# Layer norm sums by chunks on TensorE, with another order list, in a kernel of interleaved memory-attention and local-attention layers

## The chip, the core and the metric

The kernel runs on one core of one Trainium2 chip. The metric is device time in microseconds (us) from launch to the last result. The time before is the median of three runs. A profile is one execution, recorded instruction by instruction; its span runs from the first to the last instruction.

The core has TensorE (PE in the profile; its weight loads are listed apart as PEld), VectorE (DVE), ScalarE (ACT), GpSimd (POOL) and SyncE (SP), which here issues the loads of weights. Each takes its own instructions in program order and waits on semaphores for the others.

## The reference

Four layers run one after the other over a sequence of 2048 rows of 640: A, B, A, B, each on the layer norm of its input and added to it.

```python
x = x + _A_ref(_layernorm(x), A_mem0, A_Wq, A_Wk, A_Wv, A_Wo, A_seg_len)
x = x + _B_ref(_layernorm(x), B_wqkv, B_wo)
x = x + _A_ref(_layernorm(x), A_mem0, A_Wq, A_Wk, A_Wv, A_Wo, A_seg_len)
x = x + _B_ref(_layernorm(x), B_wqkv, B_wo)

def _layernorm(x, axis=-1, eps=1e-05):
    m = jnp.mean(x, axis=axis, keepdims=True)
    v = jnp.var(x, axis=axis, keepdims=True)
    return (x - m) / jnp.sqrt(v + eps)
```

Layer A walks over 64 segments of 32 rows. To each it puts 8 memory rows in front, projects these 40 rows to q, k and v with 32 heads of 192, does masked attention within the 40 rows, and projects back to 640. The first 8 rows of the result are the memory of the next segment, so the segments are a recurrence. Layer B is local attention, 32 heads of 20, each row looking at 8 rows at a distance of 2, with projections of 640 to 1920 and back.

## The kernel before

**Two lanes and steps.** Activations are kept transposed: features on the 128 partitions, in `NC` = 5 chunks, rows along the free dimension. The first pair of layers works on segment t in lane 0 while the second pair works on segment t - 2 (`LAG`) in lane 1, so one matmul serves both lanes: 80 columns in layer A (2 x 40), 64 in layer B and in a layer norm (2 x 32). `step(t)` does layer A for step t and layer B for step t - 1. There are 66 steps with layer A and a last one with layer B alone. Steps 0, 1, 64 and 65 have one lane only, and so matmuls of 40 columns.

**The list.** What a step issues, and in which order, is written out by hand in `ORDER`; every engine takes its own instructions in this order. In layer A, the heads are done in eight quads i of four heads: `Ki`, `Qi`, `Vi` are projections of 30 matmuls (L303), `KEi`, `QEi`, `VEi` bring them out of PSUM (ACT L329, DVE L335 and L337, ACT L342), `Ti` and `TEi` transpose V (PE L349, DVE L357 and L358), `Si` are the scores (L368), `Ei` the exponential (ACT L374), `EMi` the mask (DVE L380), `POi` probabilities times V (L401), `Ri` the reciprocal of the denominators (ACT L388 and L390), `OT1i` and `OT2i` the normalized output (DVE L408, L413, L414), and `Oai`, `Obi` the two halves of the projection back (15 matmuls each, L420). The last quad's projection is cut into `O7x` (chunks 0 to 2), `O7y` and `O7z` (chunks 3 and 4). Then `MEMa` and `MEMb` copy the new memory rows into `hT` for the next step (DVE L454, one for chunks 0 to 2, one for 3 and 4), and `X1` adds the residual (DVE L510).

Names that begin with a small letter are layer B of the step before: `bsq`, `bst`, `bmv`, `br`, `bap` are its layer norm; `bq`, `bk`, `bv` its projections (25 matmuls of 64 columns each, L523 and L548); `bqE`, `bkE`, `bvE` bring them out; `bs0`, `bs1`, `be0`, `be1`, `eb0`, `eb1` are scores, exponentials and masks; `bt`, `btE` transpose V; `bp`, `on` are the output and its normalization; `bo`, `boE` its transpose (PE L618 to L621, ACT L626); `by` the projection back (L634) and `byE` the residual (DVE L644, L647), which writes lane 1's input of the next step.

**The layer norms.** `LSQ`, `lst`, `LMV`, `LR`, `LAP` make layer A's layer norm for the next step, from `xin`, which `byE` and a copy on GpSimd fill. `LSQ` (`ln_sq`) works on VectorE: it squares the input (L460), sums input and squares over the five chunks in two reductions (L463), and splits the float sums into two bf16 halves, high (L465) and rest (L466). `lst` (`ln_stats`) sums these over the partitions on TensorE by two matmuls with a matrix of ones, each of 128 columns: 64 sums and 64 sums of squares. `LMV` (DVE L480, L482, L483) makes mean and variance, `LR` (ACT L490, L492) the factor, and `LAP` (DVE L500, L502 twice) applies them and writes `hT`. Layer B's `bsq`, `bst`, `bmv`, `br`, `bap` call the same functions on `x1` and write `h2T`. There are 66 of each kind in a run.

At the turn of a step, the first matmuls of `K0` need `LAP` and `MEMa`; its blocks for chunks 3 and 4 need `MEMb`.

**PSUM and weights.** Results of TensorE take four banks in turn (`big`), one pair of banks for `POi`, and two for the accumulators of the projection back. Layer A's weights are 128 pieces of 224 or 256 KB. `resident_pieces` spreads over the list which pieces are loaded anew in every step, from the list and a table of times: 79 (`N_RES`) are kept, 49 go through a ring of eight buffers (`RING`). SP issues each load where the list first uses the piece, as soon as the ring buffer is free. Layer B's weights stay; they are loaded in step 1, in four parts, behind `bst`, `bap`, `bqE` and `bvE`. Input loads and output stores sit on ScalarE's queue behind `QE0`.

```python
PIECE = (8, 7)
...
def big(self, name, shape=(P, 512), dt=F32):
    self.n_big += 1
    return self.ps_one.tile(list(shape), dt, name=name, tag=f"big{self.n_big % 4}")
```

Of the kernel before, what the change touches and what calls it, by code (L numbers as in the profile page):

```python
# [10 lines left out]
BF16 = mybir.dt.bfloat16  # L11
F32 = mybir.dt.float32
ACT = mybir.ActivationFunctionType
ALU = mybir.AluOpType
# [3 lines left out]
P = 128  # L18
D = 640
NC = 5  # L20
# [7 lines left out]
NX = 2 * SEG  # L28
# [16 lines left out]


ORDER = """
K0 Q0 bsq K0y QE0 KE0 V0 bst bmv VE0 Q1 S0 K1 T0 QE1 br bap E0 TE0 KE1 V1 S1 EM0 Q3 PO0 VE1 QE3 E1 bq T1 R0 K2
KE2 bqE TE1 Q2 K3 V2 QE2 OT10 S2 KE3 bk EM1 OT20 S3 PO1 VE2 E2 bkE Q4 T2 EM2 bs1 E3 QE4 V3 R1 K4 TE2 be1 VE3
Q5 OT11 OT21 KE4 PO2 R2 EM3 T3 eb1 bs0 be0 V4 QE5 Oa0 VE4 bv TE3 OT12 OT22 bvE Q6 S4 PO3 eb0 E4 bt R3 QE6 btE  # L50
K5 T4 EM4 K6 KE5 TE4 bp0 V5 OT13 Ob0 OT23 KE6 on0 S5 bp1 VE5 PO4 T5 Oa1 E5 R4 on1 TE5 V6 bo Q7 EM5 OT14 S6 boE
OT24 VE6 Ob1 E6 QE7 PO5 T6 EM6 TE6 by byE R5 K7 KE7 V7 S7 VE7 OT15 E7 OT25 LSQ PO6 EM7 Oa2 R6 T7 Ob2 Oa3 TE7
Ob3 OT16 OT26 Oa5 PO7 Oa6 R7 lst LMV Ob5 Oa4 Ob6 OT17 LR OT27 Ob4 LAP O7x O7y MEMa O7z MEMb X1
""".split()


# [58 lines left out]
class Kernel:  # L115
# [338 lines left out]
            nc.vector.tensor_copy(out=h[:, :, ls, 0:NM], in_=a[:, :, ls, 0:NM])  # L454

    def ln_sq(self, x):

        nc = self.nc
        sq = self.bp.tile([P, NC, NX], BF16, name="sq", tag="sq")
        nc.vector.tensor_tensor(out=sq[:], in0=x[:], in1=x[:], op=ALU.mult)  # L460
        s = self.bp.tile([P, 2, NX], F32, name="ln_s", tag="xc")
        for j, v in enumerate((x, sq)):
            nc.vector.tensor_reduce(out=s[:, j, :], in_=v[:].rearrange("p c n -> p n c"), op=ALU.add, axis=mybir.AxisListType.X)  # L463
        hl = sq[:].rearrange("p c n -> p (c n)")[:, 0:4 * NX].rearrange("p (j a n) -> p j a n", j=2, a=2)
        nc.vector.tensor_copy(out=hl[:, 0], in_=s[:])  # L465
        nc.vector.tensor_tensor(out=hl[:, 1], in0=s[:], in1=hl[:, 0], op=ALU.subtract)  # L466
        return hl

    def ln_stats(self, hl):
        nc = self.nc  # L470
        ps = self.big("ps_st")
        for j in range(2):
            nc.tensor.matmul(ps[:, 0:2 * NX], lhsT=self.ones[:], rhs=hl[:, j].rearrange("p a n -> p (a n)"), start=(j == 0), stop=(j == 1))  # L473
        return ps

    def ln_mv(self, ps):
# [201 lines left out]
    def l_piece(self, n, nt):  # L678
        x = self.xin[nt % 2]
        if n == "LSQ":  # L680
            self.asq = self.ln_sq(x)
        elif n == "lst":
            self.asp = self.ln_stats(self.asq)
        elif n == "LMV":
            self.amv = self.ln_mv(self.asp)
        elif n == "LR":
            self.amr = self.ln_r(self.amv)
        else:
            self.ln1_apply(nt)

    def b_piece(self, n, b):
        k, g = n[:2], n[2:]
        if n == "bsq":
            self.bsq = self.ln_sq(self.x1)
        elif n == "bst":
            self.bsp_ = self.ln_stats(self.bsq)
        elif n == "bmv":
            self.bmv = self.ln_mv(self.bsp_)
        elif n == "br":
            self.bmr = self.ln_r(self.bmv)  # L700
        elif n == "bap":
            self.b_ln_apply(b)
        elif n == "bq":
            self.bqp = self.b_proj(0, "ps_bq")
        elif n == "bqE":
            self.b_qE()
        elif n == "bk":
            self.bkp = self.b_proj(1, "ps_bk")
        elif n == "bkE":
            self.b_kE(b)  # L710
        elif n == "bv":
            self.b_v()
        elif n == "bvE":
            self.b_vE(b)
        elif n == "bt":
            self.b_t()
        elif n == "btE":
            self.b_tE(b)
        elif n == "bo":
            self.b_ot()  # L720
        elif n == "boE":
            self.b_oE()
        elif n == "by":
            self.b_wo()
        elif n == "byE":
            self.b_yE(b)
        elif k == "bs":
            self.b_s(int(g))
        elif k == "be":
            self.b_e(int(g))  # L730
        elif k == "eb":
            self.b_m(b, int(g))
        elif k == "bp":
            self.b_pv(int(g))
        else:
            assert k == "on", n
            self.b_on(int(g))
# [115 lines left out]
```

## Time and profile before

| what | value |
|---|---|
| median of 3 runs | 3143.12 us (3140.52 to 3145.89) |
| the profiled execution | 3140.52 us, span 3138.8 us |
| granted TensorE clock, mean of the span | 0.983 |
| DVE L463, the two reductions of a layer norm | 132 x 701 ns and 132 x some 700 ns |
| DVE L465, L466 | 226 ns and 292 ns, 132 of each |
| PE L473, matmuls with ones | 264, 128 columns each |
| weights loaded through the ring | 3234 loads of 224 or 256 KB, 3.9 to 4.0 us from issue to landing |
| HBM read | 823 MB |

A row of the profile names an engine, a line of the kernel, what is written and read, and the shape. In the timeline, a row is start, length, and the number of instructions merged into it. A matmul's recorded length includes its way through the array, so consecutive matmuls overlap in the record; what one costs in a dense stretch is the distance from start to start.

### The profile page before, as it was taken

How to read it: one execution, taken by the hardware profiler on the slowest of the kernel's cores; microseconds unless marked ns; L12 is line 12 of the kernel's file. 1: busy time of each engine (PE TensorE's matmuls, PEld its weight loads, DVE VectorE, ACT ScalarE, POOL GpSimd, SP SyncE). 2: the span in 40 equal slices, each digit the busy share in tenths (PEclk: the TensorE clock that was granted, in tenths of full speed). 3: DMA queues.
4: the chain of work that ended last, by engine and by line, in shares of the span. 5: the costliest groups of instructions: out<-in, count | busy, mean ns of one | idle time of the engine just before them, and what ended most of it. 6: DMA issues, size and time to landing. Idle time of an engine off the chain costs nothing.

```text
span 3138.8 us, 185804 instructions
## 1 busy us (share of the span) xinstructions
PE 3063.2 (98%) x83160; PEld 3036.4 (97%) x83160; DVE 2358.2 (75%) x6883; ACT 1747.2 (56%) x3829; POOL 48.2 (2%) x162
## 2 busy tenths in 40 slices
PE   6899999999999999999999999999999999999996
PEld 5799999999999999999999999999999999999996
DVE  3577777777777777777777777777777777777775
ACT  2355556555556556556555655555655655655653
POOL 2000000000000000000000000000000000000000
PEclk6899999999999999999999999999999999999998
DMA  9988888888888888888888888888888888888885
GB/s 360 320 263 267 263 262 265 264 264 265 266 268 263 268 266 263 268 266 263 268 266 261 267 263 267 261 265 268 263 267 266 264 267 267 263 269 266 262 274 184
DMA packets 487807, 838.02 MB, mean 267 GB/s; under 512 B 54240, under 2 KB 261984, under 8 KB 487008
## 3 DMA queue, kind: packets, MB, share of 16 engines
q1 hardware_dynamic: 477648, 820.89, 83.2%
q8 instruction: 651, 10.67, 1.4%
q10 hardware_dynamic: 9360, 5.26, 0.6%
q14 instruction: 148, 1.21, 0.1%
HBM read 823.31 MB, written 2.62 MB: 263 GB/s over the span
## 4 chain that ended last, share of the span: by engine, by line
PE 95%; DMA 3%; issue 1%; DVE 1%; ACT 0%; SPq 0%; DVEq 0%; ACTq 0%
PE ps_k L303 18%; PE ps_q L303 18%; PE ps_v L303 18%; PE ps_vt L349 6%; PE ps_o L401 5%; PE ps_s L368 5%; PE ps_by L634 2%; PE ps_bq L523 2%; PE ps_bv L548 2%; PE ps_bk L523 2%; DMA w_ring<-in_wA_dram 1%; PE ps_bs L575 1%; PE ps_bo L598 1%; PE ps_bvt L561 1%; PE ps_st L473 0%
## 5 line engine op out<-in xcount | busy, mean ns | idle before, releaser
L303 PEld LDWEIGHTS <-w_ring 128*128 128x128 bf16 x17754 | 784.4, 100 | 19.4 <-DMA w_ring<-in_wA_dram 10.5
L388 ACT ACTIVATE R<-ps_o 64x320 f32<-64x320 f32 (+1 forms) x1056 | 448.5, 425 | 273.8 <-PE ps_o L401 223.6
L342 ACT CAST VT_140<-ps_v 128x480 bf16<-128x480 f32 (+1 forms) x528 | 288.9, 547 | 230.7 <-PE ps_v L303 227.6
L329 ACT CAST KF_121<-ps_k 128x480 bf16<-128x480 f32 (+1 forms) x264 | 144.1, 546 | 391.2 <-PE ps_k L303 383.3
L374 ACT ACTIVATE Em<-ps_s 80x320 bf16<-80x320 f32 (+1 forms) x528 | 223.3, 423 | 157.2 <-PE ps_s L368 110.7
L420 PEld LDWEIGHTS <-w_ring 128*128 128x128 bf16 x6600 | 291.2, 100 | 3.5 <-DMA w_ring<-in_wA_dram 2.6
L335 DVE CAST QT_127<-ps_q 128x320 bf16<-128x320 f32 (+1 forms) x264 | 127.1, 481 | 203.4 <-PE ps_q L303 203.4
L357 DVE COPY Vt_134<-ps_vt 80x512 bf16<-80x512 bf16 x528 | 219.2, 415 | 71.5 <-PE ps_vt L349 69.3
L349 PE MATMUL ps_vt<-ident,VT_140 128*128 128x128 bf16 x3168 | 267.7, 221 | 0.0
L408 DVE TENSOR_TENSOR OT<-ps_o,R 128x320 bf16<-128x320 f32 (+1 forms) x528 | 249.9, 473 | 22.3 <-ACT R L390 16.6
L329 ACT CAST KF_123<-ps_k 128x480 bf16<-128x480 f32 (+1 forms) x264 | 144.1, 546 | 205.6 <-PE ps_k L303 203.9
L390 ACT ACTIVATE R<-R 128x320 f32<-128x320 f32 (+1 forms) x528 | 244.0, 462 | 16.6
L401 PE MATMUL ps_o<-Em,Vt_134 80*128 80x80 bf16 (+1 forms) x4224 | 238.0, 199 | 1.4 <-issue 1.3
L335 DVE CAST QT_125<-ps_q 128x320 bf16<-128x320 f32 (+1 forms) x264 | 126.5, 479 | 143.1 <-PE ps_q L303 71.9
L349 PEld LDWEIGHTS <-VT_140 128*128 128x128 bf16 x3168 | 191.5, 99 | 0.1
L303 PE MATMUL ps_q<-hT_92,w_ring 128*128 128x80 bf16 (+1 forms) x3234 | 185.8, 201 | 3.7 <-DMA w_ring<-in_wA_dram 2.6
L303 PE MATMUL ps_q<-hT_90,w_ring 128*128 128x80 bf16 (+1 forms) x3234 | 186.3, 201 | 2.2 <-DMA w_ring<-in_wA_dram 1.5
L401 PEld LDWEIGHTS <-Vt_134 80*128 80x128 bf16 x4224 | 181.6, 98 | 1.0 <-issue 0.7
L303 PE MATMUL ps_k<-hT_90,w_ring 128*128 128x80 bf16 (+1 forms) x3003 | 172.7, 201 | 1.4 <-DMA w_ring<-in_wA_dram 0.7
L303 PE MATMUL ps_k<-hT_92,w_ring 128*128 128x80 bf16 (+1 forms) x3003 | 171.8, 201 | 1.4 <-issue 1.4
L380 DVE TENSOR_TENSOR Em<-Em,maskA 80x320 bf16<-80x320 bf16 (+1 forms) x528 | 163.2, 309 | 12.5 <-ACT Em L374 8.4
L414 DVE TENSOR_TENSOR OT<-ps_o,R 64x160 bf16<-64x160 f32 (+1 forms) x528 | 165.1, 313 | 7.3
(3084 smaller groups left out, 8305.2 us busy)
## 6 DMA issues: line engine op xcount, KB each, us to landing
w_ring<-in_wA_dram SPq DMA_DIRECT2D x1716, 256.0 KB, 3.9
w_ring<-in_wA_dram SPq DMA_DIRECT2D x1518, 224.0 KB, 4.0
out_dram<-YT_94 ACTq DMA_DIRECT2D x32, 80.0 KB, 3.7
wqkv_sb<-in_wqkv_dram SPq DMA_DIRECT2D x3, 800.0 KB, 7.7
wo_sb<-in_wo_dram SPq DMA_DIRECT2D x1, 800.0 KB, 7.4
w_k_00_386<-in_wA_dram SPq DMA_DIRECT2D x1, 256.0 KB, 2.8
w_k_10_405<-in_wA_dram SPq DMA_DIRECT2D x1, 256.0 KB, 3.8
w_q_10_438<-in_wA_dram SPq DMA_DIRECT2D x1, 256.0 KB, 4.6
```

Source lines behind the costliest of these rows:

```text
L303: self.nc.tensor.matmul(ps[:, NT * n + c0:NT * n + c1], lhsT=self.block(kind, i, h, k), rhs=hT[:, NT * c + c0:NT * c + c1], start=(h == 0 ...
L329: self.nc.scalar.copy(out=kf[:, :, self.cs], in_=self.kp[i][:, 0:6 * NT].rearrange("p (a n) -> p a n", a=6)[:, :, self.cs])
L335: nc.vector.tensor_copy(out=qt[:, :, 0:4:3, cs], in_=pv[:, :, 0:3:2, cs])
L342: self.nc.scalar.copy(out=vt[:, :, self.cs], in_=self.vp[i][:, 0:6 * NT].rearrange("p (a n) -> p a n", a=6)[:, :, self.cs])
L349: nc.tensor.transpose(out=ps[:, n, :], in_=self.VT[:, NT * n:NT * n + P], identity=self.ident[:])
L357: nc.vector.tensor_copy(out=vt[:, :, 0:4:3, :], in_=src[:, :, 0:3:2, :])
L374: self.nc.scalar.activation(out=e[0:NT, :, cs], in_=self.sv[i][0:NT, :, cs], func=ACT.Exp, scale=float(DH) ** -0.5)
L388: self.nc.scalar.activation(out=r[rows, :, :, self.cs], in_=d, func=ACT.Ln)
L390: self.nc.scalar.activation(out=rf, in_=rf, func=ACT.Exp, scale=-1.0)
L401: nc.tensor.matmul(ov[:, pr, b, self.cs], lhsT=vt[0:NT, 512 * pr + P * b:512 * pr + P * (b + 1)], rhs=em[0:NT, 2 * pr + b // 2, self.cs], ...
L408: self.nc.vector.tensor_tensor(out=ot[:, :, 0:3:2, cs], in0=self.ov[:, :, 0:4:3, cs], in1=self.r[i][:, :, :, cs], op=ALU.mult)
L420: self.nc.tensor.matmul(self.acc[c // 3][:, o:o + self.cs.stop - self.cs.start], lhsT=self.block("o", i, h, k), rhs=ot[:, m, self.cs], sta ...
```

## The change

The change is named so: two DVE copies per quad merged away by a mask on half chunks and wider patterns; 79 resident pieces; list from remeasured DVE times. What differs between the files is this. `ln_sq` only squares. `ln_stats` does the sums over the chunks on TensorE: five matmuls of 64 columns on the input and five on the squares, each with the matrix of ones, added up in PSUM over the chunks. `ORDER` is another list of the same items. `qE`, `tE` and `N_RES` are the same in both files; which 79 pieces stay follows from the list.

```diff
 ORDER = """
-K0 Q0 bsq K0y QE0 KE0 V0 bst bmv VE0 Q1 S0 K1 T0 QE1 br bap E0 TE0 KE1 V1 S1 EM0 Q3 PO0 VE1 QE3 E1 bq T1 R0 K2
-KE2 bqE TE1 Q2 K3 V2 QE2 OT10 S2 KE3 bk EM1 OT20 S3 PO1 VE2 E2 bkE Q4 T2 EM2 bs1 E3 QE4 V3 R1 K4 TE2 be1 VE3
-Q5 OT11 OT21 KE4 PO2 R2 EM3 T3 eb1 bs0 be0 V4 QE5 Oa0 VE4 bv TE3 OT12 OT22 bvE Q6 S4 PO3 eb0 E4 bt R3 QE6 btE
-K5 T4 EM4 K6 KE5 TE4 bp0 V5 OT13 Ob0 OT23 KE6 on0 S5 bp1 VE5 PO4 T5 Oa1 E5 R4 on1 TE5 V6 bo Q7 EM5 OT14 S6 boE
-OT24 VE6 Ob1 E6 QE7 PO5 T6 EM6 TE6 by byE R5 K7 KE7 V7 S7 VE7 OT15 E7 OT25 LSQ PO6 EM7 Oa2 R6 T7 Ob2 Oa3 TE7
-Ob3 OT16 OT26 Oa5 PO7 Oa6 R7 lst LMV Ob5 Oa4 Ob6 OT17 LR OT27 Ob4 LAP O7x O7y MEMa O7z MEMb X1
+K0 bsq Q0 K0y V0 QE0 KE0 bst VE0 Q1 bmv T0 S0 K1 QE1 E0 V1 br KE1 TE0 K2 EM0 VE1 KE2 S1 PO0 bap T1 TE1 E1 EM1
+Q2 Q3 QE2 V2 QE3 S2 bq K3 R0 VE2 OT10 T2 E2 OT20 PO1 bqE V3 KE3 TE2 K4 S3 EM2 R1 bk OT11 OT21 VE3 E3 bkE Q4
+KE4 PO2 T3 QE4 TE3 V4 bs0 Q5 R2 EM3 OT12 VE4 be0 OT22 QE5 S4 Q6 PO3 K5 E4 R3 KE5 T4 QE6 bs1 bv EM4 bvE be1 TE4
+Oa0 V5 OT13 OT23 S5 PO4 eb0 VE5 bt eb1 Ob0 T5 K6 R4 Oa1 E5 btE V6 KE6 VE6 TE5 bp0 OT14 S6 OT24 EM5 on0 PO5 Ob1
+T6 bp1 E6 R5 TE6 EM6 OT15 K7 V7 Q7 VE7 OT25 KE7 on1 PO6 Oa2 T7 R6 QE7 Ob2 TE7 bo boE Oa3 S7 by E7 OT16 OT26
+EM7 Oa5 PO7 byE LSQ Ob3 lst LMV Oa4 R7 OT17 Oa6 LR OT27 Ob5 Ob4 LAP Ob6 O7x MEMa O7y O7z MEMb X1
 """.split()
...
     def ln_sq(self, x):
-
-        nc = self.nc
         sq = self.bp.tile([P, NC, NX], BF16, name="sq", tag="sq")
-        nc.vector.tensor_tensor(out=sq[:], in0=x[:], in1=x[:], op=ALU.mult)
-        s = self.bp.tile([P, 2, NX], F32, name="ln_s", tag="xc")
-        for j, v in enumerate((x, sq)):
-            nc.vector.tensor_reduce(out=s[:, j, :], in_=v[:].rearrange("p c n -> p n c"), op=ALU.add, axis=mybir.AxisListType.X)
-        hl = sq[:].rearrange("p c n -> p (c n)")[:, 0:4 * NX].rearrange("p (j a n) -> p j a n", j=2, a=2)
-        nc.vector.tensor_copy(out=hl[:, 0], in_=s[:])
-        nc.vector.tensor_tensor(out=hl[:, 1], in0=s[:], in1=hl[:, 0], op=ALU.subtract)
-        return hl
-
-    def ln_stats(self, hl):
+        self.nc.vector.tensor_tensor(out=sq[:], in0=x[:], in1=x[:], op=ALU.mult)
+        return sq
+
+    def ln_stats(self, x, sq):
         nc = self.nc
         ps = self.big("ps_st")
-        for j in range(2):
-            nc.tensor.matmul(ps[:, 0:2 * NX], lhsT=self.ones[:], rhs=hl[:, j].rearrange("p a n -> p (a n)"), start=(j == 0), stop=(j == 1))
+        for j, src in enumerate((x, sq)):
+            for c in range(NC):
+                nc.tensor.matmul(ps[:, NX * j:NX * (j + 1)], lhsT=self.ones[:], rhs=src[:, c, :], start=(c == 0), stop=(c == NC - 1))
         return ps
```

More of the change, by code (lines that the diff above doesn't have):

```diff
@@ L682, in l_piece @@
         elif n == "lst":
-            self.asp = self.ln_stats(self.asq)
+            self.asp = self.ln_stats(x, self.asq)
         elif n == "LMV":
@@ L695, in b_piece @@
         elif n == "bst":
-            self.bsp_ = self.ln_stats(self.bsq)
+            self.bsp_ = self.ln_stats(self.x1, self.bsq)
         elif n == "bmv":
```

## The prediction

> **What bounds the kernel now.** I read the busy times first, then the granted clock along the span, then the chain that ended last.
>
> ```profile
> PE 3063.2 (98%) x83160; PEld 3036.4 (97%) x83160; DVE 2358.2 (75%) x6883; ACT 1747.2 (56%) x3829; POOL 48.2 (2%) x162
> PEclk6899999999999999999999999999999999999998
> PE 95%; DMA 3%; issue 1%; DVE 1%; ACT 0%; SPq 0%; DVEq 0%; ACTq 0%
> ```
>
> TensorE carries 95% of the chain. A busy share cannot say whether it is dense, because ends of matmuls are modelled, so I took stretches of the trace, cut at the first matmul of K0 of a step.
>
> ```profile
> 138.04:3028.21 2890.17, 2883.24 (x78120) 2872.88 (x78120) 2235.18 (x6448) 1667.62 (x3596) 25.22 (x61) 1.00 0.85 265
> ...
> 1584.24:1630.67 46.43, 46.41 (x1260) 46.31 (x1260) 36.05 (x104) 26.89 (x58) 0.42 (x1) 1.00 0.87 265
> ```
>
> The columns are stretch, length, then busy time (and count) of PE, PEld, DVE, ACT and POOL, clock, DMA share and GB/s. The first row is steps 2 to 63, 62 steps with both layers: 46.62 us each. The second is one clean step, 46.43 us at full clock. VectorE needs 36.05 us of that, so ten microseconds of it are spare. So a step costs the sum of its matmul spacings, plus whatever gaps are left. Reading start to start through the timeline, I find one gap that returns in nearly every step, at its end:
>
> ```profile
> 1536.88 0.56 DVE L502 TENSOR_TENSOR hT_90<-ln_xc,ln_r 128x160 bf16<-128x160 f32 x2
> 1536.89 0.27 PE L420 MATMUL ps_acc_51495<-OT,w_ring 128*128 128x80 bf16 x3
> 1537.17 0.42 PE L420 MATMUL ps_acc_51496<-OT,w_o_11_1962 128*128 128x80 bf16 x7
> 1537.36 0.20 DVE L454 CAST hT_90<-ps_acc_51495 128x48 bf16<-128x48 f32 x1
> 1537.61 0.45 PE L303 MATMUL ps_k<-hT_90,w_k_00_386 128*128 128x80 bf16 x8
> 1537.63 0.19 DVE L454 CAST hT_90<-ps_acc_51496 128x32 bf16<-128x32 f32 x1
> ```
>
> The last seven O matmuls start at 1537.17 and at 35.8 ns each are issued by 1537.42; K0 starts at 1537.61. In the 0.19 us between, K0 waits for the memory rows (MEMa, L454 at 1537.36). MEMa's data were ready earlier: O7x was issued by 1536.99, and VectorE starts about 0.21 us after a last matmul (1537.42 to 1537.63 for MEMb). It sat behind LAP (L502, ending at 1537.44, successors starting 0.08 us early). VectorE's queue is thus late by 0.16 us at this one place.
>
> **The change, part by part.** *Added on TensorE.* A layer norm's two 128-column matmuls become ten of 64 columns, each with its own weight load. Spacings come from these rows:
>
> ```profile
> 1500.00 0.90 PE L523 MATMUL ps_bq<-h2T_371,wqkv_sb 128*128 128x64 bf16 x25
> 1500.73 0.50 PE L349 MATMUL ps_vt<-ident,VT_140 128*128 128x128 bf16 x6
> 1501.07 0.45 PE L303 MATMUL ps_k<-hT_92,w_ring 128*128 128x80 bf16 x8
> ```
>
> 25 matmuls of 64 columns take 0.73 us: 29.2 ns each. Six of 128 columns take 0.34 us: 56.7 ns each. So a layer norm goes from 0.113 to 0.292 us, +0.179. Two per step in 62 steps: +22.2 us. Bounds from the neighbours: 25.0 ns (30 matmuls of 40 columns in 0.75 us in step 64) gives +0.137 a layer norm, 17.0 us in all; 35.8 ns (80 columns) gives +0.245, 30.4 us. I take 29.2, the same shape.
>
> The rule that speaks against this part is in the Trainium skill, "TensorE: Matmul & The Clock Gate", section "LDWEIGHTS (loading the stationary operand)": a load lasts its column count over 1.2 GHz, an estimate of 107 ns here. Were eight more of them exposed per layer norm, the steady steps would lose about 106 us. The trace records loads of 98 to 100 ns too, but each of the 25 matmuls above has its own, and they still come every 29.2 ns; no load is exposed.
>
> *Removed on VectorE.* Two reductions (L463, 0.70 us each), a cast (L465, 0.23) and a subtraction (L466, 0.29). From the start of L460 to the next instruction was 2.08 us (1529.21 to 1531.29) and becomes some 0.3, so 1.8 us a layer norm, 3.6 a step. VectorE has spare time, so this pays only where its queue is late: at the step's end, and in the last step.
>
> *The step's end under the new list.* Counted from the end of by's matmuls, at 0.536 us per 15 blocks: Oa5, PO7 (0.285), Ob3, then lst at 1.36 to 1.65, five O halves to 4.33, O7x to 4.97, O7y and O7z to 5.40. VectorE: byE 0.21, LSQ 0.79 to 1.12, in time for lst's first half at 1.36. Statistics (three of 0.26) 1.86 to 2.6; ScalarE's R7 to 2.4 and LR to 3.3; OT17, OT27 from 2.63 to 3.7, before O7x at 4.33; LAP 3.7 to 4.86. MEMa then waits only for O7x: 4.97 + 0.21 = 5.18. K0 starts 0.25 us after MEMa (1537.36 to 1537.61): 5.43 against 5.40. The gap shrinks from 0.19 to 0.03: -0.16 x 62 = -9.9 us. Bounds: 0 and -11.8. What is late next is O7x itself, not VectorE; MEMb is ready at 5.86, K0's fourth chunk needs it at 6.07.
>
> *The other moves*, costed at nothing, bounds 0 and +0.3 us a step. I summed the matmul time between each producer and consumer in the new list. The shortest are bo to by, 0.82 us, which hides boE (0.20 + 0.42 + 0.07 = 0.69 by the row of L626 and its neighbours); S7 to PO7, 1.27, which hides E7 and EM7 (0.20 + 0.43 + 0.05 + 0.31 + 0.06 = 1.05); by to lst, above. Before, these three distances were 2.52, 3.31 and 6.56. If ScalarE reached boE a quarter microsecond late, by would wait some 0.1 us a step, with byE and LSQ queued behind it. A PSUM bank comes round after 1.36 us at the least, 1.19 before. The list also orders SP's weight loads: 49 of 128 pieces stream per step in both; a ring slot is released at least 5.98 us before its next use (6.08 before) and a load lands in 3.9 to 4.0. The four layer-B weight loads hang on bst, bap, bqE and bvE in step 1; from there to their use there are 9.3, 8.7, 10.6 and 13.8 us, before 5.5, 8.4, 12.2 and 11.7, against 7.7 to land. The loads and stores on ScalarE's queue keep their place after QE0.
>
> *Ends.* Steps 0 and 1 are bound by loading weights (DMA share 1.02 to 1.04 between 10 and 100 us): 0. Steps 64 and 65 have three more layer norms, +0.5, and a wait of 0.47 us at 3071.93 that should mostly go, -0.4. The last step is a chain:
>
> ```profile
> 3118.31 0.33 DVE sq L460
> 3118.63 1.21 DVE ln_s L463 x2
> 3119.86 0.24 DVE sq L465
> 3120.13 0.30 DVE sq L466
> 3120.47 0.28 PE ps_st L473
> 3120.77 0.23 DVE ln_m L480
> ```
>
> From L460 to ln_m 2.46 us. After: 0.33 for sq with the five matmuls on x beside it, 0.05, five on sq at 60 ns (25 of L523 take 1.51 us there), 0.30 to ln_m: 0.98. So -1.5.
>
> *Sum:* 22.2 - 9.9 + 0.5 - 0.4 - 1.5 = +10.9 us. The profiled execution took 3140.5 us (span 3138.8), so the same execution would take 3151.4. It was the fastest of three; the median is 2.6 above, and I predict on it: 3143.1 + 10.9 = 3154 us, own range 3149 to 3159.
>
> **The rivals.** *The gap at the step's end stays.* MEMa might wait for O7y, or LAP come late because R7 or lst slips: 3154 + 9.9 = 3164. For it: my walk leaves 0.3 us at LAP. Against: VectorE has 1.8 us less ahead of it there. *A new wait takes its place*, at bo to by or lst: 0.3 us a step, 18.6 us, 3173. For it: the distances shrank. Against: each still covers its chain. *Faster by fewer fetches.* PE's weight loads wait 41.2 us in the largest rows marked "issue" (23.2 + 7.1 + 6.5 + 4.4), with no releaser; if these are instruction fetches and half went with the 593 instructions that VectorE's list loses, 20.6 us would go: 3133. It turns the sign once over 10.9 of the 41.2 are saved, and tells from no change at 17.2. Against: TensorE's list gets 2112 more (loads and matmuls), so the total grows. *The price is not there:* ten matmuls at 25.0 ns and the whole gap gone make 17.0 - 11.8 - 1.4 = +3.8, 3147. That the change does not do what its words say is a rival only in part: the copies per quad and the 79 resident pieces stand in both files; the sums and the list are all that differs.
>
> **How the numbers follow.** Forecast 0.64, gap stays 0.17, new wait 0.10, fewer fetches 0.06, price not there 0.03. 0.2% is 6.3 us, about what a measurement of this kernel can tell from no change; so beyond 3149.4 is slower. The forecast's low end, 0.10 of it, and the last case make no change 0.13; faster is 0.06; slower the rest, 0.81. Range 3144 to 3169: it leaves out the fetch case, most of the new wait, and tails, under 0.2.
>
> **What would show it.** The clean step at 46.62 to 46.65 us; the ten statistics matmuls starting over 0.29 us; O7z to K0 within 0.05 us of dense; VectorE near 32.4 us a step. A clean step of 46.8 would mean that the gap stayed; one below 46.5 that the added matmuls cost less than their columns. The prediction is wrong if any matmul but K0's first waits in every step.

## The result and the profile after

The changed kernel takes 3154.8 us (median of four runs, 3153.97 to 3162.34) against 3143.88 us for the kernel before (3140.52 to 3145.89; four runs too, one more than ahead of the prediction). The ratio is 1.0041, with a 95% interval of 1.0023 to 1.0059: slower by 11 us. The profiled execution took 3153.97 us, its span 3152.3 us. These are the lines of its page on busy time, the granted clock along the span, and the chain by engine:

```profile
PE 3083.0 (98%) x84216; PEld 3063.0 (97%) x84216; DVE 2168.6 (69%) x6355; ACT 1740.4 (55%) x3829; POOL 44.6 (1%) x162
PEclk9999999999999999999999999999999999999998
PE 95%; DMA 3%; issue 1%; DVE 0%; ACT 0%; SPq 0%; DVEq 0%; ACTq 0%
```

In the first two slices, steps 0 and 1, the granted clock is higher than before (9 and 9 tenths for 6 and 8), and these steps are no shorter for it; in steps 2 to 63 it is 1.00 in both profiles.

TensorE has 1056 more matmuls, VectorE is busy for 190 us less, and the chain is TensorE's as before: the work went from an engine with spare time to the one that sets the end. Next the stretches, with columns as before (length, then busy time and count of each engine): steps 2 to 63, and one clean step.

```profile
140.66:3041.69 2901.03, 2894.61 (x79113) 2891.48 (x79114) 2058.37 (x5952) 1661.32 (x3596) 21.55 (x61) 1.00 0.85 264
1544.43:1591.03 46.60, 46.60 (x1281) 46.60 (x1278) 33.19 (x96) 26.79 (x58) 0.38 (x1) 1.00 0.85 265
```

The 62 steps take 2901.03 us against 2890.17 before, 10.9 us more. A clean step takes 46.60 us against 46.43 or 46.44, some 0.165 us more; over 62 steps that makes 10.2 us. So nearly all of these 10.9 us are made in the steady steps, the same amount in each. The two profiled executions lie further apart, 13.5 us (3153.97 and 3140.52): step 2 starts 2.6 us later, step 64 lasts 1.3 us longer, and what follows it is 1.3 us shorter. What a layer norm's statistics cost now is read from the timeline, from start to start (the first row is Oa5, right behind by; the second is PO7):

```profile
1538.98 0.27 PE L420 MATMUL ps_acc_51820<-OT,w_ring 128*128 128x80 bf16 x3
...
1539.51 0.46 PE L401 MATMUL ps_o<-Em,Vt_137 80*128 80x80 bf16 x8
...
1540.34 0.31 PE L466 MATMUL ps_st<-xin_86,ones 128*128 128x64 bf16 x5
1540.49 0.31 PE L466 MATMUL ps_st<-sq,ones 128*128 128x64 bf16 x5
1540.63 0.27 PE L420 MATMUL ps_acc_51820<-OT,w_ring 128*128 128x80 bf16 x3
```

From 1540.34 to 1540.63 are 0.29 us for ten matmuls, 29 ns each. At the end of the same step:

```profile
1543.15 0.56 DVE L495 TENSOR_TENSOR hT_90<-ln_xc,ln_r 128x160 bf16<-128x160 f32 x2
...
1544.14 0.42 PE L420 MATMUL ps_acc_51821<-OT,w_o_11_1969 128*128 128x80 bf16 x7
1544.17 0.21 DVE L454 CAST hT_90<-ps_acc_51820 128x48 bf16<-128x48 f32 x1 [0.46 <-PE ps_acc_51820 L420]
1544.43 0.45 PE L303 MATMUL ps_k<-hT_90,w_k_00_389 128*128 128x80 bf16 x8
```

LAP (L495) ends at 1543.71. MEMa (L454) starts at 1544.17 after 0.46 us of idle time on VectorE, and what ended that is TensorE (O7x), not VectorE's own queue. The last seven O matmuls are issued by 1544.14 + 7 x 0.0358 = 1544.39, and K0 starts at 1544.43: a gap of 0.04 us where there were 0.19.

The last step, from the chain in order of time (start, length, what):

```profile
3133.92 0.33 DVE sq L458
3134.30 0.32 PE ps_st L466 x5
3134.64 0.23 DVE ln_m L473
```

From the squares to ln_m are 0.72 us, against 2.46 before.

### The profile page after: what moved, and what is told of

Its sections match the earlier page's. It is cut to its first block, busy times and chain, and to the rows that moved or that the text cites. A ratio compares the mean times of both kernels' runs of the same rounds, so it can differ in the third digit from the quotient of the medians.

```text
span 3152.3 us, 187351 instructions
## 1 busy us (share of the span) xinstructions
PE 3083.0 (98%) x84216; PEld 3063.0 (97%) x84216; DVE 2168.6 (69%) x6355; ACT 1740.4 (55%) x3829; POOL 44.6 (1%) x162
## 3 DMA queue, kind: packets, MB, share of 16 engines
HBM read 823.31 MB, written 2.62 MB: 262 GB/s over the span
## 4 chain that ended last, share of the span: by engine, by line
PE 95%; DMA 3%; issue 1%; DVE 0%; ACT 0%; SPq 0%; DVEq 0%; ACTq 0%
PE ps_k L303 18%; PE ps_q L303 18%; PE ps_v L303 17%; PE ps_vt L349 6%; PE ps_o L401 5%; PE ps_s L368 5%; PE ps_bq L516 2%; PE ps_by L627 2%; PE ps_bv L541 2%; PE ps_bk L516 2%; PE ps_st L466 1%; PE ps_bs L568 1%; PE ps_bo L591 1%; DMA w_ring<-in_wA_dram 1%; PE ps_bvt L554 1%
## 5 line engine op out<-in xcount | busy, mean ns | idle before, releaser
L303 PEld LDWEIGHTS <-w_ring 128*128 128x128 bf16 x17292 | 760.1, 100 | 16.2 <-DMA w_ring<-in_wA_dram 12.0
L420 PEld LDWEIGHTS <-w_ring 128*128 128x128 bf16 x7062 | 304.8, 100 | 4.7 <-DMA w_ring<-in_wA_dram 3.0
L401 PE MATMUL ps_o<-Em,Vt_137 80*128 80x80 bf16 (+1 forms) x4224 | 238.0, 199 | 0.5 <-issue 0.4
L401 PEld LDWEIGHTS <-Vt_137 80*128 80x128 bf16 x4224 | 185.5, 98 | 0.8 <-issue 0.8
L303 PE MATMUL ps_k<-hT_90,w_ring 128*128 128x80 bf16 (+1 forms) x2805 | 159.9, 201 | 2.7 <-DMA w_ring<-in_wA_dram 1.5
L303 PE MATMUL ps_k<-hT_92,w_ring 128*128 128x80 bf16 (+1 forms) x2805 | 159.5, 201 | 1.1 <-issue 0.5
```

Source lines behind the costliest of these rows:

```text
L303: self.nc.tensor.matmul(ps[:, NT * n + c0:NT * n + c1], lhsT=self.block(kind, i, h, k), rhs=hT[:, NT * c + c0:NT * c + c1], start=(h == 0 ...
L401: nc.tensor.matmul(ov[:, pr, b, self.cs], lhsT=vt[0:NT, 512 * pr + P * b:512 * pr + P * (b + 1)], rhs=em[0:NT, 2 * pr + b // 2, self.cs], ...
L420: self.nc.tensor.matmul(self.acc[c // 3][:, o:o + self.cs.stop - self.cs.start], lhsT=self.block("o", i, h, k), rhs=ot[:, m, self.cs], sta ...
```

## The experiments

Seven other kernels were run, and the kernel after once more. The clean step is given as the commonest length in the profiled execution (among steps 2 to 63), from the first matmul of K0 to the next; the gap is the one at the step's end.

| kernel | clean step, us | gap, us | us, median (before beside it) | ratio to before, 95% interval |
|---|---|---|---|---|
| before | 46.44 | 0.19 | 3143.88 | |
| after | 46.60 | 0.04 | 3154.80 (3143.88) | 1.0041 [1.0023, 1.0059] |
| sums alone, list of before | 46.64 | 0.04 | 3153.41 (3139.80) | 1.0052 [1.0036, 1.0067] |
| list alone, sums of before | 47.67 | 0.04 | 3216.74 (3139.80), one run | |
| before, step's end mended | 46.28 | 0.04 | 3131.42 (3139.80) | 0.9976 [0.9965, 0.9986] |
| after, ten matmuls twice | 47.18 | 0.03 | 3183.27 (3139.80), one run | |
| before, six matmuls at lst | 46.46 | 0.04 | 3144.80 (3143.84) | 1.0011 [1.0000, 1.0023] |
| before, six matmuls at bst | 46.61 | 0.19 | 3154.06 (3143.84) | 1.0042 [1.0028, 1.0056] |
| after, layer B's sums on VectorE | 46.42 | 0.03 | 3147.25 (3143.84), one run | |
| after, again | 46.60 | 0.04 | 3157.75 (3143.84), one run | |

### The sums alone

```diff
 ORDER = """
-K0 Q0 bsq K0y V0 QE0 KE0 bst VE0 Q1 bmv T0 S0 K1 QE1 E0 V1 br KE1 TE0 K2 EM0 VE1 KE2 S1 PO0 bap T1 TE1 E1 EM1
+K0 Q0 bsq K0y QE0 KE0 V0 bst bmv VE0 Q1 S0 K1 T0 QE1 br bap E0 TE0 KE1 V1 S1 EM0 Q3 PO0 VE1 QE3 E1 bq T1 R0 K2
...
```

> The sums over chunks move to TensorE, the list stays the one of before. Theory (two terms: ten matmuls cost their columns, and the new list closes the gap at the step's end): the gap of 0.19 us stays, because the queue at the step's end is set by the place of lst, R7 and LAP in the list; a clean step of 46.43 + 0.36 = 46.79 us, some 3165 us in all. Rival (VectorE's relief closes the gap, the list does nothing): a clean step as after, 46.60 us, gap below 0.05, 3155 us.

My theory missed: 46.64 us, not 46.79, and the gap is gone under the old list. The rival's number fits better, but its reason does not fit the timeline of this run:

```profile
1542.34 0.46 PE L401 MATMUL ps_o<-Em,Vt 80*128 80x80 bf16 x8
...
1543.66 0.23 DVE L473 TENSOR_SCALAR ln_m<-ps_st 128x64 f32<-128x64 f32 x1 [1.39 <-PE ps_st L466]
...
1545.99 0.56 DVE L495 TENSOR_TENSOR hT<-ln_xc,ln_r 128x160 bf16<-128x160 f32 x2
...
1546.44 0.42 PE L420 MATMUL ps_acc<-OT,w_o 128*128 128x80 bf16 x7
1546.46 0.20 DVE L454 CAST hT<-ps_acc 128x48 bf16<-128x48 f32 x1
1546.72 0.45 PE L303 MATMUL ps_k<-hT,w_k 128*128 128x80 bf16 x8
```

MEMa still follows LAP back to back (L495 ends at 1546.55, L454 starts 0.09 us earlier, with no idle time). VectorE was no sooner: from PO7's start (L401) to MEMa's are 1546.46 - 1542.34 = 4.12 us. In the kernel before, the same two lie 4.11 us apart:

```profile
1533.25 0.46 PE L401 MATMUL ps_o<-Em,Vt_134 80*128 80x80 bf16 x8
...
1534.40 0.23 DVE L480 TENSOR_SCALAR ln_m<-ps_st 128x64 f32<-128x64 f32 x1 [1.21 <-PE ps_st L473]
...
1537.36 0.20 DVE L454 CAST hT_90<-ps_acc_51495 128x48 bf16<-128x48 f32 x1
```

What changed is TensorE's side: from PO7's start to the issue of the last of O7z it is 1546.69 - 1542.34 = 4.35 us, and was 1537.42 - 1533.25 = 4.17. lst stands between PO7 and O7z, so its 0.18 us went into the hole: the gap closed because TensorE arrives later, not because VectorE is done sooner. And VectorE idles 1.39 us ahead of ln_m here (1.21 before), so the reductions cannot have been what delayed it. The new theory: a chain PO7, R7, OT17, OT27, LAP, MEMa of 4.11 us hangs on PO7, and any TensorE work put beside it is free until the gap is filled. The kernel after agrees with it: from PO7 (1539.51) to where LAP lets VectorE go on (0.08 us ahead of its end at 1543.71) are 4.12 us, so the chain is as long without the reductions under the new list too.

### The list alone

```diff
 ORDER = """
-K0 Q0 bsq K0y QE0 KE0 V0 bst bmv VE0 Q1 S0 K1 T0 QE1 br bap E0 TE0 KE1 V1 S1 EM0 Q3 PO0 VE1 QE3 E1 bq T1 R0 K2
+K0 Q0 bsq K0y V0 QE0 KE0 bst VE0 Q1 bmv T0 S0 K1 QE1 E0 V1 br KE1 TE0 K2 EM0 VE1 KE2 S1 PO0 bap T1 TE1 E1 EM1
...
```

> The list of after with the sums of before on VectorE. Theory: the list brings lst so near to byE that it fits the short LSQ only; LSQ starts at 1539.65 in the trace after, the reductions and the split end 2.08 us later at 1541.73, lst's place on TensorE is 1540.34, so TensorE waits about 1.4 us for them in every step: a clean step of 46.60 - 0.36 + 1.4 = 47.7 us, some 3220 us. Rival (the list does nothing): 46.43 us, 3144 us. Rival (the list alone is worth its 0.17 us a step): 46.27 us, 3134 us.

As the theory said, 47.67 us. The timeline shows the wait:

```profile
1525.43 0.42 PE L420 MATMUL ps_acc<-OT,w_o 128*128 128x80 bf16 x7
1525.85 0.68 DVE L463 TENSOR_REDUCE ln_s<-sq 128x64 f32<-128x320 bf16 x1
...
1526.82 0.29 DVE L466 TENSOR_TENSOR sq<-ln_s,sq 128x128 bf16<-128x128 f32 x1
1526.84 0.54 PE L473 MATMUL ps_st<-sq,ones 128*128 128x128 bf16 x2 [0.99 <-DVE sq L465]
1527.22 0.45 PE L420 MATMUL ps_acc<-OT,w_ring 128*128 128x80 bf16 x8
```

TensorE is through with the O half at 1525.43 + 0.25 = 1525.68. The first statistics matmul waits until 1526.84 for the cast, the second for L466, and the O matmuls go on at 1527.22: 1.54 us for work of 0.11. So the new list needs the short LSQ, or it pays 1.43 us a step; the old one runs with either.

### The kernel before with its step's end mended

```diff
-... Oa5 PO7 Oa6 R7 lst LMV Ob5 Oa4 Ob6 OT17 LR OT27 Ob4 LAP ...
+... Oa5 PO7 lst LMV LXC Oa6 R7 Ob5 Oa4 Ob6 OT17 LR OT27 Ob4 LAP ...
...
+        elif n == "LXC":
+            self.axc = self.ln_xc(x, self.amv[0])
```

`LXC` is the subtraction of the mean (L500 before), and `LAP` the rest.

> The kernel before with its sums, and only the step's end mended: lst and LMV right after PO7, and the subtraction of the mean (L500) taken out of LAP and put after LMV, ahead of OT17. Theory: VectorE has 1.2 us idle ahead of LMV, so the subtraction fits there, LAP ends 0.5 us earlier, MEMa waits for O7x alone, and the gap of 0.19 us falls to 0.03: a clean step of 46.27 us, 3134 us. Rival (the gap needs VectorE to be rid of the reductions): 46.43 us, 3144 us.

It came as the theory said: a clean step of 46.28 us, and 8.4 us less than the kernel before beside it (ratio 0.9976, 0.9965 to 0.9986). The list also decides which pieces stay, and other pieces do here (HBM read 825.44 MB for 823.31); the gain in the clean step is that of the gap, 0.16 us, so nothing is left to put down to them. The end of a step there:

```profile
1576.98 0.56 DVE L507 TENSOR_TENSOR hT<-ln_xc,ln_r 128x160 bf16<-128x160 f32 x2
...
1577.86 0.42 PE L420 MATMUL ps_acc<-OT,w_o 128*128 128x80 bf16 x7
1577.89 0.21 DVE L454 CAST hT<-ps_acc 128x48 bf16<-128x48 f32 x1 [0.35 <-PE ps_acc L420]
1578.15 0.45 PE L303 MATMUL ps_k<-hT,w_k 128*128 128x80 bf16 x8
```

MEMa has 0.35 us of idle time ahead of it and waits for TensorE alone; all reductions are still on VectorE. This kernel is faster than the one before by 0.24%, and so than the one after.

### The ten matmuls twice

```diff
-            for c in range(NC):
-                nc.tensor.matmul(ps[:, NX * j:NX * (j + 1)], lhsT=self.ones[:], rhs=src[:, c, :], start=(c == 0), stop=(c == NC - 1))
+            for o in (NX * j, NX * (j + 2)):
+                for c in range(NC):
+                    nc.tensor.matmul(ps[:, o:o + NX], lhsT=self.ones[:], rhs=src[:, c, :], start=(c == 0), stop=(c == NC - 1))
```

> The kernel after with the ten matmuls of every layer norm done twice, the second time into columns that nothing reads. Theory (columns decide): 0.29 us more for each layer norm, a clean step of 46.60 + 0.58 = 47.18 us, 132 x 0.29 = 38 us more in all, 3193 us. Rival (the ten matmuls cost 25 ns each and a small wait beside them makes up the rest): 0.25 us more each, 47.10 us, 3188 us. Rival (repeated loads of the same weights are exposed): over 47.5 us.

A clean step of 47.18 us: 0.58 more for 20 matmuls, 29 ns each, as columns say. The total of the single run, 3183, lies below the 3193 that I had added up from the step; the 62 steps account for 33 us more than after (2934.36 against 2901.03), and outside of them this execution was 4 us shorter, 4.2 of it behind step 64 (61.37 against 65.59 us).

### Six more matmuls, at two places

```diff
+        for _ in range(more):
+            nc.tensor.matmul(ps[:, 4 * NX:5 * NX], lhsT=self.ones[:], rhs=hl[:, 0, 0], start=True, stop=True)
...
-            self.asp = self.ln_stats(self.asq)
+            self.asp = self.ln_stats(self.asq, 6)
```

> The kernel before with six more matmuls of 64 columns (0.175 us) ahead of layer A's statistics matmuls, into columns that nothing reads; VectorE keeps all its reductions. New theory (the gap is the slack of a chain that starts at PO7: PO7, R7, OT17, OT27, LAP, MEMa last 4.11 us before and in the run with the sums alone, while TensorE's way from PO7 to the end of O7z was 4.17 us and is 4.35 there; any matmul between the two fills the gap): the six cost next to nothing, a clean step of 46.44 to 46.47 us, gap 0.03, no change in all. Rival (the gap closed because VectorE lost the reductions): gap 0.19, a clean step of 46.62 us, 11 us more.

The second kernel has the six in `bst` (`self.ln_stats(self.bsq, 6)`) instead.

> The same six matmuls ahead of layer B's statistics, early in the step and outside the stretch from PO7 to O7z. New theory: they cost their columns, 46.44 + 0.175 = 46.62 us for a clean step, gap 0.19, 11 us more in all. Rival (the relief of VectorE closed the gap): the same for this run; so only this run and the one with the six at layer A together tell them apart.

Both came as the new theory said. At lst, the clean step is 46.46 us and the gap 0.04; at bst, 46.61 and 0.19. The end of a step of each, first with the six at lst:

```profile
1630.86 0.56 DVE L504 TENSOR_TENSOR hT<-ln_xc,ln_r 128x160 bf16<-128x160 f32 x2
...
1631.32 0.42 PE L420 MATMUL ps_acc<-OT,w_o 128*128 128x80 bf16 x7
1631.34 0.20 DVE L454 CAST hT<-ps_acc 128x48 bf16<-128x48 f32 x1
1631.60 0.45 PE L303 MATMUL ps_k<-hT,w_k 128*128 128x80 bf16 x8
```

```profile
1592.34 0.56 DVE L504 TENSOR_TENSOR hT<-ln_xc,ln_r 128x160 bf16<-128x160 f32 x2
...
1592.63 0.42 PE L420 MATMUL ps_acc<-OT,w_o 128*128 128x80 bf16 x7
1592.82 0.46 DVE L454 CAST hT<-ps_acc 128x48 bf16<-128x48 f32 x2
1593.07 0.45 PE L303 MATMUL ps_k<-hT,w_k 128*128 128x80 bf16 x8
```

In both, MEMa starts 0.48 us after LAP does (L504), back to back with it. But with the six at lst TensorE itself arrives later (0.02 us from the start of the last seven to MEMa, against 0.19), and K0 loses 0.03 us instead of 0.19. The same work costs 0.02 us a step at one place and 0.17 at the other, with VectorE's load the same; so a gap closes here without any relief of VectorE.

### Layer B's sums back on VectorE, and the kernel after again

```diff
-            self.bsq = self.ln_sq(self.x1)
+            self.bsq = self.ln_sq_v(self.x1)
...
-            self.bsp_ = self.ln_stats(self.x1, self.bsq)
+            self.bsp_ = self.ln_stats_v(self.bsq)
```

`ln_sq_v` and `ln_stats_v` are `ln_sq` and `ln_stats` of the kernel before.

> The kernel after with layer B's sums put back on VectorE (reductions and split behind X1, two matmuls of 128 columns), layer A's left on TensorE. Theory: one layer norm's 0.18 us comes back and nothing else, as bst has the projections K0, Q0 and V0 ahead of it: a clean step of 46.42 us, gap 0.04, some 11 us less than after. Rival (the reductions delay QE0 and what follows on VectorE, and TensorE waits): 46.60 us or more.

46.42 us: one layer norm's 0.18 us came back, and VectorE's longer queue behind X1 cost nothing in a clean step.

> The kernel after again, for its first two and last steps. In the first profile step 2 starts at 140.7 us (138.0 before), and step 64 lasts 45.0 us (43.7 before). If these belong to the change, they return within 0.5 us; if they are spread between executions, they move by a microsecond or more. Clean step 46.60 us either way.

Step 2 started at 141.7 us (140.7 in the first profile of after), step 64 lasted 45.25 us (44.98). Step 64 returned within 0.5 us, step 2 did not. Over all ten profiles step 2 starts between 137.9 and 145.6 us, and the three kernels that differ from before only in the layer norm's place or in idle matmuls lie at 137.9, 141.5 and 141.5. So what the change does to steps 0 and 1 stays open; it is within what these differ by. Step 64 is another matter: it lasts 43.2 to 44.3 us in the four profiles with the old list and all sums on VectorE, and 45.0 to 46.1 in the six others. So the longer step 64 may well belong to the change. Its cause is not known: the added matmuls of two layer norms account for 0.36 us of it, and the rest looks different in the two profiles of after: in the first the granted clock in step 64 was 0.92 (1.00 before), in the second it was 0.99, but stops of the weight loads with no releaser took 9.6 us there (7.5 in the first, 7.6 before). Behind step 64, 61.4 to 66.9 us follow, with no such order.

## Why the prediction was right, point by point

*What bounds.* Right: the chain is TensorE's in all of these profiles (95% of it, 89% with the list alone), and clean steps could be added up to one or two hundredths of a microsecond. VectorE's busy time in a clean step fell by 2.86 us to 33.19, not by 3.6 to 32.4, as the prediction had it; it decided nothing.

*The price of the ten matmuls.* Right: 0.29 us for ten in the profile, 0.29 for each repeated ten. No weight load is exposed, though each matmul has its own.

*The gap at the step's end.* The size was right (0.19 to 0.04, forecast 0.03), and so was the walk under the new list: counted from the end of by at 1538.98, lst started at 1.36, MEMa at 5.19 and K0 at 5.45, where it had 1.36, 5.18 and 5.43, and MEMa waits for O7x as it said. The cause was only half right. The prediction wrote "VectorE's queue is thus late by 0.16 us at this one place" and gave the closing to the shorter LSQ and the new list. The run with the sums alone shows the gap closed under the old list, with VectorE's chain from PO7 as long as before. In that list, lst's own added 0.18 us fills the hole. Under the new list, PO7 stands farther from the end of O7z (1539.51 to 1544.39, 4.88 us, against 4.17), and still by 4.70 without the added 0.18, while the chain to K0 takes 4.12 + 0.25 = 4.37. By these numbers either is enough, and the two do not add. For the list this is worked out and not run: the list alone brings its own wait.

*The new list.* With the sums on TensorE, it is therefore worth 0.04 us a step beside the sums alone (46.60 against 46.64), not 0.16. Those 0.04 us lie ahead of PO7: before, the last two O matmuls started at 1533.14 and would have been issued by 1533.21, PO7 started at 1533.25; after, PO7 follows without a gap. No run shows what holds PO7 there. The clean step adds up as 46.44 + 2 x 0.18 - 0.15 - 0.04 = 46.61, measured 46.60. The prediction had not counted this 0.04 us; the step came out 0.02 below the 46.62 that it named at the least.

*The other moves at nothing.* Right: no matmul waits in every step of after.

*The ends.* The last step's chain fell by 1.74 us, forecast 1.5. The wait at the end of step 64 did shrink: from the start of the last seven O matmuls to K0 of step 65 it is 0.44 us (3086.23 to 3086.67) and was 0.80 (3071.13 to 3071.93), 0.36 less for a forecast of 0.4. Step 64 as a whole lasts 1.3 us longer all the same, for which the prediction had no more than two layer norms, +0.36. Steps 0 and 1 were forecast at 0 and the profile shows 2.6 us more, which is of the size that profiles differ by.

*The total.* That the median came out at 3154.8 for a forecast of 3154 is in part luck. The steady steps came out 1.4 us better than summed (10.9 for 12.3), and the profiled executions differ by 13.5 us, where the prediction had 10.9. With stops of several microseconds in each execution (last section), a total cannot confirm a sum to the microsecond; the clean step can.

*The rivals.* A gap that stays and a new wait in the steps did not come. Fewer fetches: the excess of the 62 steps over 62 clean ones was 10.9 us before, 11.8 after and 14.8 after again, so no saving is seen there. VectorE has 528 fewer instructions in the profile, not 593.

## What to carry to other kernels

Where one engine is dense, added work there is priced by its spacing at the same shape, and work taken from an engine with spare time is worth nothing unless a chain that ends in a wait runs through it. Ahead of crediting a closed gap to the relief, measure both ways from their common start (here PO7): which of them moved? A gap of this kind is nearly free room for TensorE (0.02 us for six matmuls of 0.175), and shortening the other way, here by taking one subtraction out of a chain, gives the time back as a gain.

## What was not expected of the hardware

Dense matmuls stop now and then for 0.1 to 1.5 us, nearly always with no releaser in the profile ("issue", on the matmul or on its weight load). Over steps 2 to 63 the time beyond 62 clean steps makes 5 to 16 us an execution (5.1 with the list alone, 15.6 with layer B's sums on VectorE), and it differs between two executions of one kernel (11.8 and 14.8 us for after). It is a part of why single totals differ by several microseconds, and why the clean step tells apart what totals do not. What causes the stops is not known.
